# A gated S5 layer on one core: the state kept at every token in place of every second one

## The chip, the cores and the metric

The kernel runs on one core of a Trainium2 chip, in bfloat16 with float32 sums. The core has five engines, each with its own queue that is worked off in order: TensorE (PE, matrix products; PEld is its loading of weights), VectorE (DVE), ScalarE (ACT), GpSimd (POOL) and SyncE (SP, which here issues nearly all DMAs). Waits between engines go by semaphores. The metric is the device time of one execution in microseconds, as the median over several runs.

## The reference

One sequence of 2048 tokens with 448 channels is normalised, goes through a diagonal complex state space (448 complex states), and is gated by a two-layer network with 1792 hidden units.

```python
dt = jnp.exp(log_dt)
Lam_bar = jnp.exp(dt * Lam)
B_bar = ((Lam_bar - 1.0) / Lam)[:, None] * Bmat
Bu = jnp.einsum("bld,pd->blp", x + 0j, B_bar)
h = jnp.zeros_like(Bu[:, 0, :])
for t in range(L):
    h = Lam_bar[None, :] * h + Bu[:, t, :]
    hs.append(h)
hseq = jnp.stack(hs, 1)
y = 2.0 * jnp.einsum("blp,dp->bld", hseq, Cmat).real + x * Dskip[None, None, :]
...
y = _layernorm(x, axis=-1)
h = _gelu(jnp.einsum("bsd,df->bsf", y, w1) + b1)
return jnp.einsum("bsf,fd->bsd", h, w2) + b2
...
xn = _layernorm(x, axis=-1)
s = _A_ref(xn, ...)
g = _silu(_B_ref(xn, ...))
return x + s * g
```

## The kernel before, in words

The tokens are worked in NG = 4 groups of 512, each of two blocks of 256. A group has these stages.

- Norms. VectorE takes mean and variance of each token; `ln_apply` writes the rows `xn_sb` (for the state space) and `xn2_sb` (normalised twice, for the network), and `xt` transposes them, by DMA transposes on SP's queue, into `xnT` and `xn2T`, with the channels on the partitions. The first block of group 0 goes through TensorE instead.
- State inputs, `bu` (L648). The state is kept at every second token only: NK = 256 steps a group, each fed by two tokens, so 2 × 448 = 896 rows in 7 tiles. The input matrix holds B beside Lam·B, which `lb` builds on VectorE with `combine` (L583 to L594), and seven DMA transposes from on-chip memory (`bt`) turn it into `BT`. Per group 49 matmuls at L652; ScalarE moves the sums to `u_sb` (L656 to L660).
- States, `ssm` (L666). The 448 complex states lie on 128 partitions as three tiles with a real and an imaginary part, and the last 64 states as one tile whose halves are the two parts. The rotation of each state is taken out by tables of sines and cosines `WT`, so that what is left is a real recurrence: multiply by the table (L669 to L673), seven scans (L677), cast the result to bfloat16 on ScalarE (L681 to L684), turn it back into `h_sb` (L705 to L709). GpSimd carries the last state over to the next group (L691 to L703).
- Network. `mm1` (L718) is the first layer: 14 tiles of 128 hidden units, 512 tokens wide, in matmuls of 64 rows, two of which are in the array at a time (L726); gelu on ScalarE (L736). In group 0 the first layer runs by blocks of tokens, `mm1_half` (L740), in 112 matmuls of 128 rows and 256 columns (L746), the bias as an extra row of the weights. `mm2` (L756) is the second layer: for each 128 tokens 14 matmuls (L760), then the bias b2 added by VectorE (L763) and silu by ScalarE (L764).
- Output, `ym` (L782). For each 128 tokens of one parity. Even tokens, from the state one step back: seven products with `CZ` (L795) and four with the direct matrix `M0` (L798), which holds the token's own input and the skip term. Odd tokens: seven products with `CQ` (L795, L801), and the skip term `xd`, worked out by `skip` (L766) on VectorE or GpSimd, added by VectorE (L808). Then the gating t3 = s·g (L810), the addition of x (L813), both on VectorE, and a store for each block. `CQ` and `CZ` come from C by `combine`, `M0` from products of CQ and B (`m0`, L628 to L644).

The program is recorded as a list of tasks by a helper, `Plan`. It finds the dependencies, and issues the tasks in an order written out by hand (`ORDER`), each on its engine's queue; for a task recorded by `either`, which has two possible engines, the list `SECOND` says where the second is taken. PSUM banks are fixed in the code.

Of the kernel before, what the change touches and what calls it, by code (L numbers as in the profile page):

```python
# [7 lines left out]
ACT = mybir.ActivationFunctionType  # L8
# [9 lines left out]
class Task:  # L18
# [3 lines left out]
    __slots__ = ("eng", "ins", "reads", "writes", "sem", "idx", "deps", "chain", "alts", "tag")  # L22

    def __init__(self, eng, ins, reads, writes, sem):
        self.eng, self.ins, self.reads, self.writes, self.sem = eng, ins, tuple(reads), tuple(writes), sem
        self.deps = set()
        self.chain = False
        self.tag = None
        self.alts = [(eng, ins)]

    def choose(self, k):
        self.eng, self.ins = self.alts[k]
        if self.sem in ENGS:
            self.sem = self.eng


class Plan:
# [4 lines left out]
    def __init__(self, nc):  # L42
        self.nc = nc
# [19 lines left out]

    def add(self, eng, ins, reads=(), writes=(), dur=0.2, lat=0.1, prio=0.0, sem=None, chain=False, table=None, mode=None):
        if callable(ins):
            ins = [ins]
        t = Task(eng, ins, reads, writes, sem or eng)
        t.chain = chain
        if self.tag is not None:
            t.tag = self.tag  # L70
            self.named[self.tag] = t
            self.tag = None
        self.tasks.append(t)
        return t

    def either(self, first, second, reads=(), writes=(), prio=0.0, chain=False):

        t = self.add(first[0], first[1], reads, writes, chain=chain)
        t.alts.append((second[0], second[1] if isinstance(second[1], list) else [second[1]]))
        return t  # L80

    def dma(self, eng, out_ap, in_ap, reads=(), writes=(), prio=0.0, nbytes=0, transpose=False, dur=0.45):
# [8 lines left out]
        return self.add(eng, fn, reads, writes, sem=sem)  # L91
# [20 lines left out]
    def emit(self):  # L112
# [5 lines left out]
        assert len(order) == len(set(order)) == len(self.tasks)  # L118
        done = {}
# [26 lines left out]

    def settle(self, names):
# [14 lines left out]
ST 0 18 22 10 88 1 19 16 23 15 20 2 21 11 3 9 27 12 26 24 8 17 14 13 25 5 7 6 89 4 28 90 96 91 29 45 30 97 92 98 93 31 46 47 94 99 48 63 103  # L162
95 32 53 100 49 54 101 50 102 33 51 52 114 64 44 106 65 55 38 108 116 56 105 115 39 107 57 109 40 117 58 118 41 120 42 119 36 110 122 34 121
111 37 144 124 35 104 123 43 60 112 62 125 59 B0 126 DH 72 113 67 B1 296 68 69 128 B2 70 127 300 298 73 B3 151 130 129 299 191 148 132 303
131 149 297 134 133 301 302 150 304 136 152 135 142 155 138 66 156 143 153 140 154 137 157 271 139 71 146 308 305 74 165 76 75 141 306 61
309 145 79 307 166 268 82 272 163 BF 83 77 310 86 169 164 181 158 277 269 159 401 180 400 270 170 167 398 147 160 274 W0 W1 W2 405 168 404
182 399 W3 171 280 402 403 183 161 406 172 H10 173 275 162 H11 192 278 184 281 356 174 H12 175 357 185 358 311 78 410 360 80 176 81 H13 361
312 411 229 407 412 408 362 230 409 501 502 H15 363 500 314 188 231 359 315 504 383 189 506 503 H16 232 505 507 508 H14 186 368 178 364 369
187 233 509 365 179 512 366 234 H21 513 177 237 316 H20 367 238 460 313 239 458 510 461 235 242 190 246 373 243 459 245 514 195 193 196 511
236 247 H24 244 H23 194 199 251 466 85 197 200 84 464 198 203 87 249 252 201 253 240 202 241 205 248 204 317 370 206 215 262 217 207 382 318  # L170
218 257 216 258 319 208 254 259 250 D0 263 255 260 209 320 371 256 264 321 210 219 221 D1 220 211 223 265 266 273 222 376 267 413 374 322
224 212 225 D2 326 276 213 227 226 379 325 279 228 214 D3 327 282 331 465 333 323 283 414 285 375 377 332 380 H26 415 334 467 H22 O00 335
470 324 484 462 471 328 289 330 284 416 339 329 286 340 463 261 341 342 H30 290 343 344 417 337 336 292 515 548 418 O01 345 H25 351 516 346
549 H31 485 347 287 348 468 288 293 349 H33 350 550 372 352 338 554 419 378 353 518 354 294 384 291 420 295 421 469 385 387 422 551 423 517
O10 555 388 574 391 389 424 519 428 386 427 475 392 429 437 394 435 425 520 472 426 390 430 436 431 521 432 476 473 481 522 438 O11 433 381
523 440 395 482 447 393 478 434 448 524 575 439 441 442 443 449 450 453 444 451 445 525 446 355 479 452 H32 526 454 H34 455 552 396 556 553
456 397 529 457 H36 557 H35 530 560 531 558 561 539 527 538 559 486 565 483 474 528 487 536 477 535 489 480 534 532 562 537 541 O20 566 533
540 493 488 542 563 544 567 490 564 568 491 494 492 543 545 496 569 546 571 570 O21 495 547 581 572 497 573 578 498 576 O30 499 577 582 579
583 580 584 585 593 589 586 594 595 587 588 590 591 596 592
""".split()]  # L180
SECOND = [int(k) if k.isdigit() else k for k in """
142 143 144 157 163 167 171 173 195 201 219 223 308 309 407 411 413 416 484 485 508 509 512 515 516 518 519 575 W0 W1 W2 595
""".split()]

# [10 lines left out]
def bass_recurrent_scan__ssm_conv_s5__mixer_channel_mlp__prompt_kernel(  # L195
# [14 lines left out]
    NB, NG, NF, NK = 8, 4, 14, 256  # L210
# [3 lines left out]
    with ExitStack() as es:  # L214
        def SB(name, shape, dtype=BF):
# [5 lines left out]
        iota = SB("iota", [128, NK], F32)  # L221
        sgn = SB("sgn", [128, 4], F32)
        cw = SB("cw", [128, 40, 4], F32)
# [3 lines left out]
        dcol = SB("dcol", [128, 8], F32)  # L227
        x_all = SB("x_all", [128, NB, 2, D])
        w1_sb = SB("w1_sb", [128, 4, F])
        w2_sb = SB("w2_sb", [128, NF, D])  # L230
        b1b = SB("b1b", [128, NF])
        b1f = SB("b1f", [128, NF], F32)
        Bn = SB("Bn", [128, 7, 896])
        BT = SB("BT", [128, 7, 7, 128])
        Cr = SB("Cr", [128, 7, D])
        CQ = SB("CQ", [128, 7, D])
        CZ = SB("CZ", [128, 7, D])
        M0 = SB("M0", [128, 4, D])
        dbc = SB("dbc", [128, D])
        xd = SB("xd", [128, 4, D])  # L240
        xr = SB("xr", [128, 2, D], F32)
# [3 lines left out]
        o2 = SB("o2", [128, 4, D], F32)  # L245
        WT = SB("WT", [128, 4, 3, NK])
        xn_sb = SB("xn_sb", [128, 2, 896])
        xn2_sb = SB("xn2_sb", [128, 2, 1024])
        xnT = SB("xnT", [128, 2, 7, 256])
# [8 lines left out]
        pb = SB("pb", [128, 3, 2, NK])  # L258
        v_sb = SB("v_sb", [128, 4, 2, NK])
        s_f = SB("s_f", [128, 4, 2, NK], F32)  # L260
        s_b = SB("s_b", [128, 4, 2, NK])
        h_sb = SB("h_sb", [128, 2, 7, NK + 2])
        Cs = h_sb[0:112, 1, :, :].rearrange("p k c -> p (k c)")[:, 18:530]
# [8 lines left out]
        (LRE, LIM, LDT, DT, F1, A1, R1, R2, F2, DEN, RDEN, LR, LI, NLI, T0, T1, QR, QI, NQR, NQI, ZR, ZI, NZR, NZI,  # L272
         T2, ZT) = range(26)
# [4 lines left out]
        def pool(fn, reads=(), writes=(), dur=0.3, prio=0):  # L278
            kb.add("pool", fn, reads, writes, dur=dur, lat=0.15, prio=prio)

        def dve(fn, reads=(), writes=(), dur=0.2, prio=0):
            kb.add("dve", fn, reads, writes, dur=dur, lat=0.12, prio=prio)

        def act(fn, reads=(), writes=(), dur=0.6, prio=0, table=None):
            kb.add("act", fn, reads, writes, dur=dur, lat=0.2, prio=prio, table=table)

        def pe(fn, reads=(), writes=(), dur=0.2, prio=0):
            kb.add("pe", fn, reads, writes, dur=dur, lat=0.25, prio=prio)

        with nc.Block():  # L290

            S0 = -100
# [636 lines left out]
```

## Time and profile before

| what | us |
|---|---|
| median of 3 runs (range) | 154.56 (154.44 to 154.69) |
| span of the profiled execution | 153.0 |
| TensorE busy | 148.4 |
| VectorE busy | 122.0 |
| ScalarE busy | 110.9 |
| GpSimd busy | 34.8 |

The span is the profiler's, from the first to the last event of the program in that execution; the difference to the median, about 1.5 us, is start and end outside it. The profile names an operation by its line in the code, with its output and inputs: `L677 DVE TENSOR_TENSOR_SCAN` is the scan of line 677 on VectorE. In a group's row stand the count, the sum of busy time, the mean of one in ns, and the engine's idle time ahead of it with what ended it. The clock row (PEclk) gives TensorE's granted clock in tenths.

### The profile page before, as it was taken

The page shows a single profiled execution, that of the slowest core. Times are in us where ns is not written, and L with a number is a line of the kernel's source. Part 1 is how long each engine was busy: PE and PEld are TensorE (multiplying, and loading weights), DVE is VectorE, ACT ScalarE, POOL GpSimd, SP SyncE. Part 2 cuts the span into 40 slices and gives each one's busy share as a digit, 9 for nine tenths or more (in the row PEclk, how much of TensorE's full clock was granted, in tenths as well). Part 3 has the DMA queues.
Part 4 walks back from the last instruction along what each step waited for, and adds up shares of the span by engine and source line. Part 5 has one row for each costly group of instructions (what it writes and reads, how often), then busy time and mean ns, then how long its engine had stood idle before and what let it go on. Part 6 is the DMA issues. An engine that isn't in the chain of part 4 may idle for free.

```text
span 153.0 us, 2971 instructions
## 1 busy us (share of the span) xinstructions
PE 148.4 (97%) x1055; PEld 88.2 (58%) x1055; DVE 122.0 (80%) x262; ACT 110.9 (72%) x190; POOL 34.8 (23%) x115
## 2 busy tenths in 40 slices
PE   7899999999999999999999999999999999999992
PEld 2599965455555555665544456755666555555551
DVE  5785989998957999899898864494976972999564
ACT  3867769999959988699999999832294789661100
POOL 6467491073000060310004310210006000000241
PEclk9999999999999999999999999999999999999999
DMA  4999986999989770000020221131300100001022
GB/s 114 297 324 366 252 185 118 177 125 227 196 143 121 140 137 0 4 0 0 2 50 14 42 78 60 27 38 27 95 4 0 60 0 0 4 0 62 0 107 73
DMA packets 31512, 14.04 MB, mean 92 GB/s; under 512 B 25733, under 2 KB 31113, under 8 KB 31498
## 3 DMA queue, kind: packets, MB, share of 16 engines
q1 hardware_dynamic: 31344, 13.79, 40.1%
q8 instruction: 8, 0.13, 0.3%
q10 hardware_dynamic: 154, 0.07, 0.2%
q14 instruction: 6, 0.05, 0.1%
HBM read 6.20 MB, written 1.84 MB: 53 GB/s over the span
## 4 chain that ended last, share of the span: by engine, by line
PE 94%; DVE 2%; DMA 1%; issue 0%; DVEq 0%
PE psum L760 28%; PE psum L726 21%; PE psum L652 14%; PE psum L795 13%; PE psum L746 8%; PE psum L798 4%; PE psum L631 3%; DMA x_all<-in_A_x_dram 1%; PE psum L801 1%; DVE lnst L395 1%; PE psum L636 1%; PE psum L403 1%; PE psum L466 0%; DVE xn2T L407 0%; DVE t L810 0%
## 5 line engine op out<-in xcount | busy, mean ns | idle before, releaser
L760 PE MATMUL psum<-w_sb,gT 128*128 128x448 bf16 x224 | 44.5, 353 | 0.0
L726 PE MATMUL psum<-xn2T,w_sb 64*128 64x512 bf16 x294 | 33.5, 378 | 0.0
L760 PEld LDWEIGHTS psum<-w_sb,gT 128*128 128x128 bf16 x224 | 21.8, 98 | 19.5 <-issue 0.2
L736 ACT ACTIVATE gT<-psum,b1f 128x512 bf16<-128x512 f32 x42 | 25.9, 690 | 3.1 <-PE psum L726 3.1
L726 PEld LDWEIGHTS psum<-xn2T,w_sb 64*128 64x128 bf16 x294 | 15.6, 109 | 16.3 <-issue 2.3
L652 PE MATMUL psum<-xnT,BT 128*128 128x256 bf16 x196 | 24.1, 273 | 0.0
L652 PEld LDWEIGHTS psum<-xnT,BT 128*128 128x128 bf16 x196 | 18.5, 98 | 6.4 <-issue 3.1
L677 DVE TENSOR_TENSOR_SCAN s_f<-cw,cur,v_sb 128x256 f32<-128x256 f32 x21 | 15.1, 740 | 0.2
L451 ACT ACTIVATE xn_sb<-x_all,lnw 128x448 bf16<-128x448 bf16 (+1 forms) x21 | 13.4, 667 | 1.2 <-POOL lnw L428 1.2
L764 ACT ACTIVATE g_sb<-o 128x448 bf16<-128x448 f32 x16 | 8.9, 572 | 6.4 <-DVE o L763 6.2
L746 PE MATMUL psum<-xn2T,w_sb 128*128 128x256 bf16 x112 | 12.7, 273 | 0.4 <-DVE xn2T L407 0.4
L746 PEld LDWEIGHTS psum<-xn2T,w_sb 128*128 128x128 bf16 x112 | 11.9, 111 | 0.9 <-issue 0.8
L795 PE MATMUL psum<-CZ,h_sb 128*128 128x448 bf16 x56 | 11.9, 353 | 0.0
L810 DVE TENSOR_TENSOR t<-psum,g_sb 128x448 bf16<-128x448 f32 (+2 forms) x10 | 5.7, 574 | 7.6 <-PE psum L798 3.8
L656 ACT ACTIVATE u_sb<-psum 128x512 bf16<-128x512 f32 x12 | 7.1, 593 | 5.9 <-PE psum L652 5.8
L763 DVE TENSOR_TENSOR o<-psum,b2bc 128x448 f32<-128x448 f32 x16 | 9.7, 614 | 1.5 <-PE psum L760 1.5
L795 PE MATMUL psum<-CQ,h_sb 128*128 128x448 bf16 (+2 forms) x54 | 10.5, 332 | 0.0
L752 ACT ACTIVATE gT<-psum 128x512 bf16<-128x512 f32 x14 | 8.2, 593 | 3.2 <-PE psum L746 3.1
L381 DVE BATCH_NORM_STATS2 lnst<-x_all 128x6 f32<-128x448 bf16 x14 | 8.3, 610 | 0.6 <-DMA x_all<-in_A_x_dram 0.5
L590 ACT ACTIVATE tmp<-Cr,cw 128x448 f32<-128x448 bf16 (+1 forms) x12 | 7.9, 672 | 1.0 <-DVE CQ L593 0.9
L691 POOL TENSOR_TENSOR cwk<-s_f,ang 128x3 f32<-128x3 f32 x3 | 1.1, 352 | 32.6 <-DVE s_f L677 32.5
L795 PEld LDWEIGHTS psum<-CZ,h_sb 128*128 128x128 bf16 x56 | 5.4, 98 | 4.9 <-issue 0.4
(157 smaller groups left out, 212.0 us busy)
## 6 DMA issues: line engine op xcount, KB each, us to landing
out_dram<-tmp SPq DMA_DIRECT2D x7, 224.0 KB, 1.9
x_all<-in_A_x_dram SPq DMA_DIRECT2D x3, 448.0 KB, 4.5
w_sb<-in_B_w_dram SPq DMA_DIRECT2D x3, 448.0 KB, 6.6
w_sb<-in_B_w_dram SPq DMA_DIRECT2D x3, 384.0 KB, 4.6
Bn<-in_A_B_im_dram SPq DMA_DIRECT2D x1, 336.0 KB, 9.3
Bn<-in_A_B_re_dram SPq DMA_DIRECT2D x1, 336.0 KB, 9.8
x_all<-in_A_x_dram SPq DMA_DIRECT2D x2, 112.0 KB, 2.1
x_all<-in_A_x_dram SPq DMA_DIRECT2D x1, 224.0 KB, 3.7
```

Source lines behind the costliest of these rows:

```text
L381: dve([lambda e, b=b, par=par, q=q: e.bn_stats(lnst[:, q, :], x_all[:, 2 * g + b, par, :])], [f"x{2 * g + b}"] + (["xmT0p1"] if (g, b) == ...
L451: ("act", [lambda e, o=o, i=i: e.activation(o, i, ACT.Identity, bias=nb, scale=rs) for o, i in pairs], 0.75, 0.2)]
L652: fns = [lambda e, r=r, m=m, d=d: e.matmul(psum[:, 4, r * NK:(r + 1) * NK], BT[:, m, d, :], xnT[:, gx, d, :], start=(d == 0), stop=(d == 6 ...
L677: dve(lambda e, i=i, ri=ri, init=init: e.tensor_tensor_scan(s_f[:, i, ri, :], col(R2, i).to_broadcast([128, NK]), v_sb[:, i, ri, :], init, ...
L726: return lambda e: e.matmul(psum[:, b0 + k, :], w1_sb[halves[h], d, fcol(2 * j + k)], rhs[halves[h], d, :, :], start=first and d == 0, sto ...
L736: act([lambda e, k=k: e.activation(gT[:, gb, 2 * j + k, :], psum[:, b0 + k, :], ACT.Gelu_apprx_tanh, bias=b1f[:, 2 * j + k:2 * j + k + 1]) ...
L746: fns = [lambda e, k=k, d=d: e.matmul(psum[:, banks[k], :].rearrange("p (r c) -> p r c", r=2)[:, :, cs], w1_sb[:, d, fcol(2 * j + k)], rhs ...
L752: act(lambda e: e.activation(gT[:, 0, 2 * j:2 * j + 2, :].rearrange("p k (r c) -> p k r c", r=2)[:, :, :, cs], psum[:, b0:b0 + 2, :].rearr ...
L760: fns = [lambda e, fi=fi: e.matmul(psum[:, bk, 0:D], gT[:, gb, fi, q * 128:(q + 1) * 128], w2_sb[:, fi, :], start=(fi == 0), stop=(fi == N ...
L763: dve(lambda e: e.tensor_tensor(o2[:, ob, :], psum[:, bk, 0:D], b2bc[:], ALU.add), [f"ps{bk}", "b2bc"], [f"oo{ob}"], 0.62, prio - 76)
L764: act(lambda e: e.activation(g_sb[:, gs, :], o2[:, ob, :], ACT.Silu), [f"oo{ob}"] + (["silu"] if g == 0 else []), [f"g{gs}"], 0.58, prio - ...
L795: fns = [lambda e, k=k: e.matmul(psum[:, bk, c0:c1], h_sb[:, hb, k, k0:k0 + 128], cm[:, k, c0:c1], start=(k == 0), stop=False) for k in ra ...
```

## The change

The state is kept at every token: NK = 512 steps a group. With that there is no Lam·B (`lb`), no second output matrix `CZ`, no `M0`, and no separate skip term: every block of 128 tokens has seven products with `CQ` and four small ones with a diagonal matrix `DG` (128 columns each), which add the skip term in PSUM. The recurrence uses R1, the decay of one token, in place of R2.

```diff
-    NB, NG, NF, NK = 8, 4, 14, 256
+    NB, NG, NF, NK = 8, 4, 14, 512
...
-                fns = [lambda e, k=k: e.matmul(psum[:, bk, c0:c1], h_sb[:, hb, k, k0:k0 + 128], cm[:, k, c0:c1], start=(k == 0), stop=False)
-                       for k in range(7)]
-                if par == 0:
-                    fns += [lambda e, d=d: e.matmul(psum[:, bk, c0:c1], xnT[:, gx, d, xs], M0[:, d, c0:c1], start=False, stop=(d == 3)) for d in range(4)]
...
+                    fns = [lambda e, k=k: e.matmul(psum[:, bank.b, c0:c1], h_sb[:, hb, k, k0:k0 + 128], CQ[:, k, c0:c1], start=(k == 0), stop=(k == 6))
+                           for k in range(7)]
+                    ds = [d for d in range(4) if c0 <= d * 128 < c1]
+                    fns[1:1] = [lambda e, d=d: e.matmul(psum[:, bank.b, d * 128:min(D, d * 128 + 128)], xnT[:, gx, r * 4 + d, xs], DG[:, d, 0:min(128, D - d * 128)],
+                                                        start=False, stop=False) for d in ds]
```

The state inputs have 448 rows in place of 896, in four tiles of rows. For the three full tiles the matmuls are of 64 rows and 512 columns, two in the array at a time, as in the first layer (a shared helper, `halved`); the fourth tile of channels holds its 64 rows twice, so that each half has them, for which `xn_sb` and `x_all` are padded to 512 columns (extra loads `ldxe`, and copies on GpSimd, `dup`). The last 64 states' inputs are two halves of the array's columns, real and imaginary, over all rows.

```diff
+            def halved(out, wt, rhs, n, tag, rd, bank):
+                def half(k, d, h):
+                    first = h == k
+                    return lambda e: e.matmul(out(k), wt(k, d, halves[h]), rhs(k, d, halves[h]),
+                                              start=first and d == 0, stop=not first and d == 2)
+                own = [half(k, d, k) for d in range(4) for k in range(2)]
+                other = [half(k, d, 1 - k) for d in range(3) for k in (1, 0)]
...
+                    def colhalf(d, k):
+                        h = slice(0, 128 if d < 3 else 64)
+                        return lambda e: e.matmul(psum[halves[k], bank.b, :], BT[h, d, k * D + 384:k * D + D], xr[h, d, :, :], start=(d == 0), stop=(d == 3))
+                    pe([colhalf(d, k) for d in range(4) for k in range(2)], rd, [bank.key], rows(4, 512))
```

B is transposed by six DMA transposes, four straight from HBM and two for its last 64 columns from a buffer `Bs`, after a copy on GpSimd.

```diff
+            def bt():
+                for n in range(2):
+                    for ri, bm in enumerate((A_B_re, A_B_im)):
+                        kb.dma("sp", BT[:, 0:3, ri * D + n * 224:ri * D + n * 224 + 224], dram_ap(bm, n * 224 * D, [[D, 224], [1, 384]]),
+                               writes=[f"BT{ri}{n}"], nbytes=172032, transpose=True)
+                for ri in range(2):
+                    tail = Bs[:, ri, :].rearrange("p (t c) -> p t c", t=4)
+                    pool(lambda e, tail=tail: e.tensor_copy(tail[:, :, 64:128], tail[:, :, 0:64]), [f"Bs{ri}"], [f"Be{ri}"], 0.45)
+                    kb.dma("sp", BT[:, 3, ri * D:ri * D + D].rearrange("p (t r) -> p t r", t=4), Bs[:, ri, :], reads=[f"Bs{ri}", f"Be{ri}"], writes=[f"BT{ri}2"], nbytes=114688, transpose=True)
```

The first layer of group 0 uses `halved` too (196 matmuls of 64 rows and 256 columns), with its bias in the activation. The addition of x is recorded with two engines for every block; `SECOND` puts 14 of the 17 on GpSimd (17, as the last 128 tokens are split in two parts).

```diff
-                fns = [lambda e, k=k, d=d: e.matmul(psum[:, banks[k], :].rearrange("p (r c) -> p r c", r=2)[:, :, cs],
-                                                    w1_sb[:, d, fcol(2 * j + k)],
-                                                    rhs[:, d, :, :], start=(d == 0), stop=(d == 3))
-                       for k in range(2) for d in range(4)]
...
+                halved(lambda k: psum[:, bank.b + k, :].rearrange("p (r c) -> p r c", r=2)[:, :, cs], lambda k, d, h: w1_sb[h, d, fcol(2 * j + k)],
+                       lambda k, d, h: xr[h, d, :, :], 256, f"H0{j}{b}", (["xmT0p0", "xmT0p1"] if b == 0 else ["xmT0_1"]) + [f"w1_{c}", f"w1r_{c}"], bank)
...
-                    if last and par:
-                        kb.either(*on, rd, [f"o{ob}_{par}_{c0}"], prio)
-                    else:
-                        dve(add, rd, [f"o{ob}_{par}_{c0}"], on[0][2], prio)
...
+                    on = [("dve", add, 0.15 + 0.25 * w / D), ("pool", add, 0.2 + 1.0 * w / D)]
+                    kb.either(*on, rd, [f"o{ob}_{r}_{c0}"])
```

Several buffers share memory now: the table of token numbers lies in `pb`, the tail of B in `s_b`, C in `h_sb`. The buffer of second-layer sums, `o2`, has two places in place of four. PSUM banks are handed out by a list, `BANKS`, in the order of first use, with the waits that follow from it (`place`). A block's rows are contiguous tokens now, not alternate ones. `ORDER` has 593 tasks in place of 640 and is new throughout, as are `SECOND` and `BANKS`.

More of the change, by code (lines that the diff above doesn't have):

```diff
@@ L118, in emit @@
         assert len(order) == len(set(order)) == len(self.tasks)
+        self.place(order)
         done = {}
@@ L716, in fcol, with mm1 @@
                 return slice(a * 128 + fi - a, (a + n) * 128, n)
[L718 removed]
+            def mm1(g, j):
                 gx, gb = g % 2, g % 2
[L720 to L736 removed]
@@ L831, in bass_recurrent_scan__ssm_conv_s5__mixer_channel_mlp__prompt_kernel @@
-            P = {"ln": -9, "bu": -8, "mm1": 0, "mm2": 5, "ym": 6}
-            def pr(k, g, x=0.0):
-                return P[k] + 10 * g + x
+                if r and not last:
+                    kb.dma("sp", dram_ap(out, off, [[D, 128], [256 * D, 2], [1, D]]), o_sb[:, ob, :].rearrange("p (r d) -> p r d", r=2),
+                           reads=[f"o{ob}_0_0", f"o{ob}_1_0", f"o{ob}_1_256"], writes=[f"out{g}{b}"], nbytes=229376)
+            idle = kb.psum()
+            kb.tag = "I0"
+            pe([lambda e: e.matmul(psum[:, idle.b, :], still[:, :], still[:, None, :].to_broadcast([128, 4, 128]), start=True, stop=True) for _ in range(8)],
+               ["still"], [idle.key], 3.4)
```

823 lines of the change are left out of this document (384 added, 439 removed), and 3 rows, old and new, of the table ORDER.

## The prediction

> **What bounds the kernel now.** I read the page's totals first, then the two kinds of busy rows by slice, then the chain that ended last.
>
> ```profile
> span 153.0 us, 2971 instructions
> PE 148.4 (97%) x1055; PEld 88.2 (58%) x1055; DVE 122.0 (80%) x262; ACT 110.9 (72%) x190; POOL 34.8 (23%) x115
> PE   7899999999999999999999999999999999999992
> DVE  5785989998957999899898864494976972999564
> PEclk9999999999999999999999999999999999999999
> PE 94%; DVE 2%; DMA 1%; issue 0%; DVEq 0%
> PE psum L760 28%; PE psum L726 21%; PE psum L652 14%; PE psum L795 13%; PE psum L746 8%; PE psum L798 4%; PE psum L631 3%; DMA x_all<-in_A_x_dram 1%; PE psum L801 1%; DVE lnst L395 1%; PE psum L636 1%; PE psum L403 1%; PE psum L466 0%; DVE xn2T L407 0%; DVE t L810 0%
> ```
>
> TensorE is busy in every slice but the first and the last, at full granted clock, and holds 94% of the chain: its matmuls end to end are the time. VectorE is 31.0 us short of the span and has slack in the slices with 4 to 7. Whatever leaves TensorE shortens the kernel, until VectorE, with 80%, has more than its slack put on it. Both happen here.
>
> **TensorE, part by part.** The chain's pieces (start, us) give what a matmul takes of the path.
>
> ```profile
> 7.22 5.40 PE psum L746 x48
> 12.62 0.45 PE psum L466 x8
> 13.06 7.11 PE psum L746 x64
> 41.19 3.13 PE psum L726 x28
> 60.70 1.32 PE psum L631 x7
> 70.38 0.79 PE psum L636 x14
> 73.92 1.32 PE psum L795 x7
> 105.41 0.76 PE psum L652 x7
> 124.93 0.87 PE psum L652 x7
> 149.92 0.12 PE psum L801
> ```
>
> The direct matrix M0 goes: three products of 1.32 and one of 0.79, −4.75. The output stage now takes 13+4+1% of 153.0, 27.5 us. After, each of 16 blocks is seven matmuls, 1.32, and four diagonal ones of 128 columns (0.45/8 = 0.056 each), 0.22: 16 × 1.54 = 24.7, −2.8. The first layer of group 0 takes 5.40 + 7.11 = 12.51; it becomes 196 half-row matmuls of 256 columns. No such row exists; L636, halves of 224 columns, takes 0.79/14 = 56 ns, the half-row of 512 columns 3.13/28 = 112 ns. So 56 ns, 11.0 us, −1.5; if two halves did not share the array it would be 111 ns (7.11/64), 21.8 us, +9.2. L726 and L636 both show the sharing, so I keep 56. The state inputs are 28 runs of seven at 0.76 to 0.87, 21.3 to 24.4, and their share of 14% says that they stand at the low end, some 22; after, per group 42 half-row matmuls and 8 column halves at 112 ns, 5.6, in all 22.4: I take +0.2. The column halves have only L636 for a row; unshared they would add 8 × 0.11 = 0.9 a group. Each change from half rows back to the full array costs 0.87 − 0.76 = 0.11. Sum: −4.75 − 2.8 − 1.5 + 0.2 = −8.9. Were TensorE still the bound, the span would be 144.1.
>
> **VectorE, part by part.** The state pass now handles 512 steps a group where it handled 256.
>
> ```profile
> L669 DVE TENSOR_TENSOR pa<-u_sb,WT 128x1536 bf16<-128x1536 bf16 x4 | 3.8, 955 | 2.2 <-ACT u_sb L656 2.1
> L672 DVE TENSOR_TENSOR pa<-u_sb,WT 128x512 bf16<-128x512 bf16 x4 | 1.7, 416 | 2.7 <-ACT u_sb L660 2.7
> L677 DVE TENSOR_TENSOR_SCAN s_f<-cw,cur,v_sb 128x256 f32<-128x256 f32 x21 | 15.1, 740 | 0.2
> 129.67 2.03 DVE L677 TENSOR_TENSOR_SCAN s_f<-cw,cur,v_sb 128x256 f32<-128x256 f32 x3
> L563 DVE SCALAR_TENSOR_TENSOR s_f<-iota,cw,s_f 128x256 f32<-128x256 f32 x4 | 1.7, 474 | 0.0
> L566 DVE SCALAR_TENSOR_TENSOR s_f<-s_f 128x1024 f32<-128x1024 f32 x1 | 1.2, 1224 | 0.0
> L763 DVE TENSOR_TENSOR o<-psum,b2bc 128x448 f32<-128x448 f32 x16 | 9.7, 614 | 1.5 <-PE psum L760 1.5
> L593 DVE SCALAR_TENSOR_TENSOR CZ<-Cr,cw,tmp 128x448 bf16<-128x448 bf16 x7 | 4.7, 679 | 0.0
> L593 DVE SCALAR_TENSOR_TENSOR Bn<-Bn,cw,tmp 128x448 bf16<-128x448 bf16 x7 | 4.7, 671 | 0.0
> L808 DVE TENSOR_TENSOR xr<-psum,xd 128x448 f32<-128x448 f32 x7 | 4.3, 611 | 2.9 <-PE psum L801 2.9
> ```
>
> Six wide operations a group go from 1536 to 3072 elements: the slope (955 − 416)/1024 gives 0.526 ns an element, so 0.955 + 0.81 = 1.76. The scan: fixed part from L563 and L566, 474 − 256 × 0.977 = 224 ns; the rest of 740, 516 ns, doubles: 1.26 (bounds 0.74 and 1.48). Three scans in 2.03 stand 0.645 apart, so 512 steps stand about 1.16 apart; neighbours overlap by 0.06 to 0.1 us in general. The small pair of operations becomes 0.69 and 0.42. That is per group 6 × 0.8 + 7 × 0.52 + 0.4 = 8.9 more, 35 in all. Removed: the 14 combines for CZ and Lam·B with most of their scaled copies (9.4 and more), the skip sums (4.3), and 14 adds that go to GpSimd (next part). VectorE comes to some 133 to 135 us of work, as much as TensorE's, and unlike TensorE's it is a chain with a start: no state pass can begin before the first state inputs.
>
> [...]
>
> **The start of that chain.** B now comes by six transposes on SP's queue, behind the transposes of the normalised rows.
>
> ```profile
> 19.65 1.33 SPq L89 DMA_TRANSPOSE xnT<-xn_sb  x1
> 26.08 2.59 SPq L89 DMA_TRANSPOSE BT<-Bn  x2
> 30.22 3.46 SPq L89 DMA_TRANSPOSE BT<-Bn  x2
> BT<-Bn SPq DMA_TRANSPOSE x7, 3.9
> L656 ACT ACTIVATE u_sb<-psum 128x512 bf16<-128x512 f32 x12 | 7.1, 593 | 5.9 <-PE psum L652 5.8
> ```
>
> One transpose of B goes ahead; then SP stands at the first transpose of normalised rows until they are ready, 19.65 now, and I take 20.0. Behind it stand three of B, the second block's rows and the last two of B: six issues of 1.30 (2.59/2) later, at 27.8, the last one goes out and lands 3.9 after that, 31.7. The last two state-input tiles (28 halves, 3.1) need it, and their evacuation by ScalarE (two of 0.593) follows: VectorE's first wide operation starts at 36.0. TensorE has the first layer and the second of group 0 up to about 29 meanwhile, so 31.7 is SP's doing. At 3.46 for two, the bound above, the last lands 3 us later, and so does all that follows. The two transposes of the tail also wait for GpSimd's copies, small and early; behind all of them on SP stand group 1's rows, C's transposes and the extra 64-column loads of x, which the combines and the first output block need only after the scans.
>
> From there to the last state of group 3, VectorE in its new order executes 24 wide operations at 1.70 net of overlap (40.8), 28 scans at 1.16 (32.5), 8 of 0.63 and 8 of 0.38 (8.1), 10 gatings like L810 and 8 b2 adds like L763 at 0.54 (9.7), 7 combines at 0.60 (4.2), and 1.9 of normalisation: 97.2. ScalarE's cast of the scans, twice its size, lies in each group beside 3 us and more of gatings, b2 adds and the small scan; I cost it at nothing, and if that cover is gone it is some 3 us a group. So 36.0 + 97.2 = 133.2 if VectorE never waits.
>
> **What the adds cost on GpSimd.** The add of x moves there for 14 of 17 pieces (16 blocks, the last in two). The rows that show both engines at once:
>
> ```profile
> 98.52 0.62 DVE L810 TENSOR_TENSOR t<-xr,g_sb 128x448 bf16<-128x448 f32 x1
> 98.66 1.38 POOL L775 TENSOR_TENSOR xd<-xn_sb,dbc 128x448 bf16<-128x448 bf16 x1 [9.86 <-DVE xr L808]
> 99.18 1.10 DVE L813 TENSOR_TENSOR tmp<-t,x_all 128x448 bf16<-128x448 bf16 x1
> L813 DVE TENSOR_TENSOR tmp<-t,x_all x15: 366/383/1104, 82.2 to 149.6; 128x448 bf16<-128x448 bf16 x15
> 144.62 1.09 POOL L775 TENSOR_TENSOR xr<-xd,g_sb 128x448 f32<-128x448 bf16 x1 [23.33 <-ACT g_sb L764]
> 144.74 0.62 DVE L808 TENSOR_TENSOR xr<-psum,xd 128x448 f32<-128x448 f32 x1
> 114.56 0.53 POOL L700 TENSOR_TENSOR cwk<-cwk,ang 128x1 f32<-128x1 f32 x1 [14.52 <-ACT cwk L699]
> 116.21 0.19 POOL L702 TENSOR_TENSOR cwk<-s_f,ang 128x1 f32<-128x1 f32 x1
> ```
>
> The add at 99.18, median 0.383, took 1.10, and ended within 0.3 us of GpSimd's product: it stood still until GpSimd let go, 0.72 lost. The one at 144.74, which reads PSUM, lost nothing. The other way round GpSimd's small product took 0.53 beside a scan, 0.19 alone. So an add on GpSimd, about 1.0 alone, delays the VectorE operation with two SBUF operands that is issued after it. In the new order 10 of the 14 adds fall before the last state, and by their places about 8 stand ahead of a wide operation or a scan, the others ahead of operations on PSUM. At 0.8 each (0.72 and the next one's start) that is 6.4; GpSimd's 30 small products for the carried state add 0.7, by two or three that meet a wide operation at the 0.53 − 0.19 of L700. On GpSimd's own queue the carry products stand behind adds too, at up to three adds, but the scan that reads the carry comes after three wide operations (5.1), which cover it. Bounds: 0, and 10 × 1.0 + 30 × 0.1 = 13. I take 7.1, since the only row with the same operands has a price near the full one: last state at 140.3.
>
> [...]
>
> **The end.** After the last state, four output blocks on TensorE (1.54 each, 6.2 with the last one split), then what follows TensorE's last matmul now: 153.0 − 150.04 = 3.0. 140.3 + 6.2 + 3.0 = 149.5. The runs' median lies 1.5 over the profiled span (154.56 − 153.0): **151.0 us, 2.3% faster**, with VectorE and not TensorE as the bound.
>
> **The rivals.** B, the lock is hidden: adds on GpSimd fall in VectorE's waits. Then 133.2 + 9.2 = 142.4 for VectorE, under TensorE's 144.1; with 1.4 us of changes of array mode and waits for the first transposes, 145.5 and a median of 147.0. For it: L808's undisturbed 0.62, and slack in slices of 4 to 7. Against: VectorE has little slack left.
>
> C, slower: the lock at its full price. All 10 adds and the 30 small products delay VectorE, 13 us in place of 7.1: 133.2 + 13 + 9.2 + 1.5 = 156.9. It decides as soon as VectorE loses over 10.7 us, by this or by a late cast that waits behind a locked scan. For it: 1.10 at 99.18, and six wide operations of 1.76 a group that can meet an add. Against: L808's 0.62.
>
> D, the prices themselves: scans at the bound of 1.48 give 28 × 0.22 = 6.2 more, 157.2; half rows not shared give more than that. Against: L563's fixed part and L636. It has the same sign as C and is held with it.
>
> E, the change does not bring its 8.9 us on TensorE because TensorE waits in every group for states, and ends with VectorE where it did: 154.5.
>
> **How the numbers follow.** Forecast 0.45 (149 to 154), B 0.23, C with D 0.26, E 0.06. About 0.2% (0.3 us) is what a measurement of this kernel can tell from no change. Faster: forecast and B, less the upper edge, 0.66. Slower: C, D and half of E, 0.29; the rest, 0.05, same. The range reaches down to B's 147.0 less the uncertainty of its waits, 146.5, and up to D, 157.5.
>
> **What would show it.** Right: TensorE below 95% with idle time before its output blocks, released by VectorE's states; VectorE's lines heading the chain; wide operations of 1.76 and scans near 1.26; the first wide one near 36, the last small state add near 140; wide operations and scans longer than their median whenever an add runs on GpSimd, and that add well over 1 us. Wrong: the state inputs over 5.7 us a group or the half rows of 256 columns over 56 ns (TensorE's sum); the first wide operation later than 38 (SP's queue); scans near 1.48; an add on GpSimd that leaves VectorE's medians alone (then B); VectorE idle before the state operations, waiting for ScalarE's cast (then the cover I gave it is missing).

## The result, and the profile after

| | median us | span of the profiled execution | ratio to before, 95% interval |
|---|---|---|---|
| before (4 runs beside it) | 154.62 | 153.0 | |
| changed | 166.22 (164.67 to 168.11) | 162.9 | 1.0646 (1.056 to 1.0731) |

The changed kernel is 6.5% slower. Two of the four runs of the changed kernel (167.32 and 168.11, against 164.67 and 165.12) and the profiled one of the first experiment (161.62, against 158.41 to 158.65) count as slow, and the ratios leave such runs out. First its page, the totals and the rows by slice, then the chain's shares.

```profile
span 162.9 us, 3030 instructions
PE 143.9 (88%) x1140; PEld 77.5 (48%) x1140; DVE 140.0 (86%) x195; ACT 121.9 (75%) x184; POOL 75.0 (46%) x120
PE   7674599992999999999999899899995999999492
DVE  2860179986569998999999999999999999999984
PEclk9969999999699999999999999999999999999999
DMA  5633899347998790000038300000810010001013
DVE 54%; PE 10%; SPq 8%; ACT 8%; DMA 7%; POOL 5%; issue 5%; DVEq 0%; ACTq 0%
```

Two things are to be seen. From slice 13 on VectorE is full and holds 54% of the chain, as the prediction had it: the bound has moved from TensorE to VectorE. But ahead of that, in slices 1 to 12 (up to 49 us), VectorE isn't full, and stands nearly still from 12 to 20 us; TensorE is at 4 to 7 tenths up to slice 5 and at 2 in slice 10, where the kernel before had it at 9 from its third slice on. The time by stage shows which of the two is the miss. VectorE's rows for the first wide operation and the last small state sum, on its timeline (start, us):

```profile
48.25 1.76 DVE L700 TENSOR_TENSOR pa<-u_sb,WT 128x3072 bf16<-128x3072 bf16 x1 [0.29 <-ACT u_sb L683]
153.13 0.42 DVE L742 TENSOR_TENSOR h_sb<-pa 128x512 bf16<-128x512 bf16 x1
```

| stage | predicted us | measured us |
|---|---|---|
| until VectorE's first wide operation | 36.0 | 48.25 |
| from there to the last state | 97.2 + 7.1 = 104.3 | 153.55 − 48.25 = 105.3 |
| from there to the end | 9.2 | 162.9 − 153.55 = 9.35 |

So 12.25 of the 13.4 us between the predicted span, 149.5, and the measured one lie ahead of the first wide operation. The 7.1 in the second row is the price of what the prediction calls the lock: time that VectorE's operations lose beside GpSimd's additions and small products (0.72 us for the addition at 99.18 in the kernel before). The chain of waits in the first stage (start, us):

```profile
4.60 2.83 SPq L107
7.47 2.68 SPq L107
10.20 1.51 SPq L107
11.75 8.29 DMA w_sb<-in_B_w_dram
21.16 3.13 ACT gT L767 x8
24.29 0.11 ACT ang L560
24.48 0.85 POOL ang L551
29.38 2.28 POOL ang L556
32.61 0.37 POOL s_b L643
33.61 0.34 POOL s_b L643
34.23 1.28 SPq L106
36.88 3.63 DMA xnT<-xn_sb
```

And SP's rows for the loads of w1, the first transpose of B and the last one, on its timeline:

```profile
2.18 10.83 SPq L107 DMA_DIRECT2D w_sb<-in_B_w_dram  x8
22.88 3.12 SPq L106 DMA_TRANSPOSE BT<-in_A_B_re_dram  x1
39.58 1.28 SPq L106 DMA_TRANSPOSE BT<-in_A_B_im_dram  x1
```

The chain reads: SP takes 2.83 and 2.68 us over two issues, where the loads ahead of them took 0.42 to 0.70; a piece of w1 lands only at 20.04; TensorE and so the gelus are late; behind eight gelus on ScalarE stands one step of 0.2 us for the sine polynomial, which runs at 24.2; GpSimd works off the ten steps of the polynomial from 24.5 until 32.0, and behind that, in its queue, stand the two copies of B's tail (L643), which end at 33.0 and 34.0. SP waits 4.5 us with a transpose for the first copy, until 33.0, and with it wait all the transposes behind; the second copy is ready by the time that SP comes to it. Two causes are in this chain: a slow load, and a short copy in a long queue.

### The profile page after: what moved, and what is told of

Its sections match the earlier page's. It is cut to its first block, busy times and chain, and to the rows that moved or that the text cites. A ratio compares the mean times of both kernels' runs of the same rounds, so it can differ in the third digit from the quotient of the medians.

```text
span 162.9 us, 3030 instructions
## 1 busy us (share of the span) xinstructions
PE 143.9 (88%) x1140; PEld 77.5 (48%) x1140; DVE 140.0 (86%) x195; ACT 121.9 (75%) x184; POOL 75.0 (46%) x120
## 4 chain that ended last, share of the span: by engine, by line
DVE 54%; PE 10%; SPq 8%; ACT 8%; DMA 7%; POOL 5%; issue 5%; DVEq 0%; ACTq 0%
DVE s_f L708 17%; PE psum L666 6%; SPq L107 6%; DMA w_sb<-in_B_w_dram 5%; DVE pb L739 5%; DVE pa L738 5%; DVE h_sb L740 4%; ACT gT L755 4%; DVE pa L700 4%; DVE t L807 4%; DVE v_sb L702 3%; DVE pb L701 3%; PE psum L801 3%; DVE CQ L633 2%; DVE o L786 2%
## 5 line engine op out<-in xcount | busy, mean ns | idle before, releaser
L666 PE MATMUL psum<-xn2T,w_sb 64*128 64x512 bf16 (+1 forms) x490 | 46.7, 342 | 8.2 <-DMA w_sb<-in_B_w_dram 6.3
L666 PEld LDWEIGHTS psum<-xn2T,w_sb 64*128 64x128 bf16 x490 | 28.1, 110 | 25.2 <-DMA w_sb<-in_B_w_dram 6.6
L809 POOL TENSOR_TENSOR tmp<-t,x_all 128x448 bf16<-128x448 bf16 x14 | 23.1, 1665 | 31.9 <-issue 17.6
L708 DVE TENSOR_TENSOR_SCAN s_f<-cw,cur,v_sb 128x512 f32<-128x512 f32 x21 | 29.4, 1448 | 0.1
L801 PE MATMUL psum<-CQ,h_sb 128*128 128x448 bf16 (+2 forms) x119 | 24.9, 342 | 2.7 <-DVE h_sb L742 2.7
L666 PE MATMUL psum<-xnT,BT 64*128 64x512 bf16 x168 | 21.1, 395 | 4.0 <-DMA xnT<-xn_sb 3.1
L787 ACT ACTIVATE g_sb<-o 128x448 bf16<-128x448 f32 x16 | 9.0, 572 | 11.2 <-DVE o L786 11.1
L767 ACT ACTIVATE gT<-psum,b1f 128x256 bf16<-128x256 f32 x28 | 11.1, 484 | 8.0 <-PE psum L666 8.0
L713 ACT ACTIVATE s_b<-s_f 128x3072 bf16<-128x3072 f32 x4 | 11.2, 2788 | 6.0 <-DVE s_f L708 6.0
L683 ACT ACTIVATE u_sb<-psum 128x1024 bf16<-128x1024 f32 x12 | 11.9, 1046 | 2.5 <-PE psum L666 2.5
L499 ACT ACTIVATE xn_sb<-x_all,lnw 128x512 bf16<-128x512 bf16 x16 | 12.7, 815 | 0.2
L807 DVE TENSOR_TENSOR t<-psum,g_sb 128x448 bf16<-128x448 f32 (+2 forms) x17 | 9.9, 585 | 0.6 <-PE psum L801 0.5
L786 DVE TENSOR_TENSOR o<-psum,b2bc 128x448 f32<-128x448 f32 x16 | 9.4, 609 | 0.0
```

The costliest lines, as they stand in the source:

```text
L499: ("act", lambda e: e.activation(dst, src, ACT.Identity, bias=nb, scale=rs), 0.81)]
L666: return lambda e: e.matmul(out(k), wt(k, d, halves[h]), rhs(k, d, halves[h]), start=first and d == 0, stop=not first and d == 2)
L683: act(lambda e: e.activation(u_sb[:, i, :, :], psum[:, bank.b:bank.b + 2, :], ACT.Copy), [bank.key], [f"u{i}"], 1.02)
L708: dve(lambda e, i=i, ri=ri, init=init: e.tensor_tensor_scan(s_f[:, i, ri, :], col(R1, i).to_broadcast([128, NK]), v_sb[:, i, ri, :], init, ...
L713: act(lambda e: e.activation(s_b[:, 0:3, :, :], s_f[:, 0:3, :, :], ACT.Copy), SF, ["sb"] + early, 2.76)
L786: dve(lambda e: e.tensor_tensor(o2[:, ob, :], psum[:, bank.b, 0:D], b2bc[:], ALU.add), [bank.key, "b2bc"], [f"oo{ob}"], 0.62)
```

## The experiments

**The load that reads its source twice, and the copies.** The changed kernel loads the last 64 rows of w1 into both halves of the partitions by one load whose source has a first dimension of 2 with step 0. The first experiment puts two plain loads of 64 rows in its place; the matmuls then wait for both, in lines that are not printed here.

```diff
-                ld("sp", w1_sb[:, 3, a:a + w], dram_ap(B_w1, 384 * F + a, [[0, 2], [F, 64], [1, w]]), [f"w1r_{c}"], 128 * w * 2, dur=0.55)
+                ld("sp", w1_sb[0:64, 3, a:a + w], dram_ap(B_w1, 384 * F + a, [[F, 64], [1, w]]), [f"w1r_{c}"], 64 * w * 2)
+                ld("sp", w1_sb[64:128, 3, a:a + w], dram_ap(B_w1, 384 * F + a, [[F, 64], [1, w]]), [f"w1s_{c}"], 64 * w * 2)
```

> The last 64 rows of w1 are loaded by two plain loads of 64 rows for each chunk in place of one load that reads its source twice. Theory of the late start, first half (the load that reads its source twice is slow and holds SP's queue: two of its neighbours' issues take 2.83 and 2.68 us, and TensorE waits 6.3 us for w1): TensorE's first layer ends near 20 in place of 26.8, ScalarE's step of the sine polynomial runs near 17 in place of 24.2, GpSimd's copies of B's tail end near 26.5 in place of 34, the first wide operation starts near 42 in place of 48.2; span near 156.5, time near 158.3. Rival, the half-row matmuls or the number of loads set that end: first layer still ends past 25, span within 1 us of 162.9. Rival, the time is lost in VectorE's stretch (the lock): the start may move, but the span stays above 160.

Measured: first wide operation at 43.56, 158.65 us, ratio 1.0228 (1.0136 to 1.032). TensorE's first layer ends at 20.6, ScalarE's step runs at 17.9, GpSimd's copies end at 27.7, and SP's last transpose of B goes out at 33.26, 6.3 earlier than in the changed kernel. The start came within 1.6 of what the theory had and the time within 0.4; both rivals fall. The start is that of the profiled execution, which took 161.62: its granted clock was 0.968 in the mean, and its 42 half rows of state inputs took 7.90, where four other versions, at 0.995 to 1.000, took 4.95. So the 4.7 us by which the start came earlier is less than what the load costs.

The second moves GpSimd's copies of B's tail (tasks 155 and 157 of `ORDER`) ahead of the polynomial (55).

```diff
-53 54 55 56 62 H001 254 ...
+53 54 155 157 55 56 62 H001 254 ...
```

> GpSimd's two copies of B's tail stand ahead of the ten steps of the sine polynomial in place of behind them; nothing else. Theory of the late start, second half (SP stands 4.5 us at a transpose that waits for a copy queued behind that polynomial): SP's transposes go on at 28.5 in place of 33.0, the first wide operation starts near 43.7 in place of 48.2, span near 158.4, time near 160.2. Rival, another wait takes its place (ScalarE's tables, which end near 40, or VectorE's norms): start moves by less than 1.5 us and the span stays above 161.4.

Measured: first wide operation at 45.82, span 159.8, 162.33 us, ratio 1.045 (1.0356 to 1.0543). SP no longer stands at the transpose of the tail. Its timeline in the changed kernel, where the transpose that begins at 33.01 waited for 4.5 us:

```profile
27.28 1.23 SPq L106 DMA_TRANSPOSE xnT<-xn_sb  x1
33.01 1.19 SPq L106 DMA_TRANSPOSE BT<-s_b  x1
```

and here:

```profile
27.51 1.23 SPq L106 DMA_TRANSPOSE xnT<-xn_sb  x1
28.86 1.20 SPq L106 DMA_TRANSPOSE BT<-s_b  x1
```

So the copies did cost SP 4.4 us; 2.4 of them reached VectorE's start. The start came 2.1 later than the theory had and the time 2.1 higher, between theory and rival. What bounds it there is TensorE: its first layer still waited for w1, the second layer of group 0 ends only at 37.7, and the evacuation of the state inputs by ScalarE at 45.6. Both edits together:

> Both edits together. Theory of the late start: what the prediction had wrong is the start alone, so with both out of the way the first wide operation starts near 37, as the prediction had it (36.0), the stretch from there to the last state stays near 105 us, and the span comes to 151.7, time near 153.5, about 0.7% under the kernel before. Rival, ScalarE's tables or TensorE's second layer bound the start at 40 or later: span 155 or more, time 156.7. Rival, the lock grows with more overlap: the stretch takes 108 us or more.

Measured: first wide operation at 38.78, the stretch to the last state 106.1, span 154.2, 155.77 us, ratio 1.0035 (0.9993 to 1.0077), which is no difference from the kernel before. The theory's start of 37, span of 151.7 and time of 153.5 were missed by about 2 us each. The two edits give back 9.5 of the 12.25 us. By the ratios, the load alone takes off 4.2 points, the copies alone 2.0, both 6.1: within the intervals they add up. The rest of the start, 2.8, was not in the theory (more on it below).

**Why that load is slow.** One load of the same bytes from 128 different rows.

```diff
-... dram_ap(B_w1, 384 * F + a, [[0, 2], [F, 64], [1, w]]) ...
+... dram_ap(B_w1, 320 * F + a, [[F, 128], [1, w]]) ...
```

> The changed kernel with one edit: the load of w1's last rows is one load of 128 different rows (320 to 447) in place of one that reads 64 rows twice; the same bytes, packets and number of loads. The lower half of that tile then holds other rows of w1, so the first layer is not the reference's. Theory: the load that reads its source twice has 2 as its outermost count and so keeps only 2 of the 16 DMA engines busy (the DMA row shows 1 to 2 tenths there). Then TensorE's wait of 6.3 us for w1 falls under 2, the long issues of 2.83 and 2.68 us on SP go, and the start and the time are as with two loads: first wide operation near 43.5, span near 158.3. Rival, the bytes or the size of the packets make it slow: the wait stays at 6 us and the span within 1 us of 162.9.

The busy times by stretch for the changed kernel and, below it, for this run (columns: TensorE, its loading, VectorE, ScalarE, GpSimd with counts, granted clock, DMA share, GB/s):

```profile
7.43:10.15 2.72, 0.83 (x10) 0.64 (x11) 2.34 (x14) 1.06 (x1) 2.33 (x12) 0.86 0.14 46
10.15:13.03 2.88, 2.33 (x22) 1.43 (x18) 1.00 (x3) 0.51 (x2) 1.21 (x4) 0.54 0.63 175
```

```profile
7.43:10.15 2.72, 2.72 (x52) 2.43 (x48) 2.34 (x14) 2.50 (x6) 2.33 (x12) 1.00 1.09 329
10.15:13.03 2.88, 2.88 (x52) 2.54 (x50) 2.20 (x6) 2.88 (x8) 0.99 (x4) 1.00 1.08 368
```

While SP was held for 2.68 us, the DMA engines were busy to 0.14, about 2 of 16, and moved 46 GB/s; in the same stretch of the run with 128 rows, in which later loads are under way already, the share is 1.09, at 329 GB/s. TensorE's first layer, by form, before and after the edit:

```profile
L666 PE MATMUL psum<-xn2T,w_sb 64*128 64x256 bf16 x196 | 13.1, 291 | 6.3 <-DMA w_sb<-in_B_w_dram 6.3
```

```profile
L674 PE MATMUL psum<-xn2T,w_sb 64*128 64x256 bf16 x196 | 11.2, 270 | 0.0
```

The wait of 6.3 us is gone. The half rows take 270 ns in place of 291: in the changed kernel the granted clock was 0.50 from 9.40 to 12.82, and the slowest of them took 417. Time 155.99, ratio 1.0077 (1.0057 to 1.0098), first wide operation at 39.72. VectorE's row for it, and SP's for the loads of w1, first with two loads a chunk and then here:

```profile
2.20 7.14 SPq L107 DMA_DIRECT2D w_sb<-in_B_w_dram  x12
```

```profile
2.20 4.03 SPq L107 DMA_DIRECT2D w_sb<-in_B_w_dram  x8
39.72 1.76 DVE L708 TENSOR_TENSOR pa<-u_sb,WT 128x3072 bf16<-128x3072 bf16 x1
```

The start is 3.8 us earlier than with two loads, and the expectation of 158.3 was too high. Four issues fewer account for 2.0 of the 3.8: SP reaches the first transpose of normalised rows at 18.94 in place of 20.98. For the rest there is the lower clock of that profiled execution (0.968 in the mean, 0.989 here), whose half rows of state inputs took 7.90 in place of 6.52 here.

This is the largest single effect on record. With nothing but the access pattern changed, and the copies left where they were, the start moves from 48.25 to 39.72, 8.5 of the 12.25 us, the span from 162.9 to 154.7, and the time gives back 5.7 of the 6.5 points. So the lateness of the copies follows for the most part from the load: the polynomial starts at 16.1 in place of 24.5, though SP still stands 3.7 us for the first copy.

That the bytes don't make the load slow is shown, for they are equal, and the wait went from 6.3 us to 0.0; nor does reading the same rows twice, for the two plain loads of the first experiment read them twice as well, and there too the wait fell, to 1.5. What is left is the pattern, a first dimension of 2 with step 0. No run separates the count of 2 from the step of 0: the theory's choice of the count was the author's estimate, which the share of 0.14, 2.2 of 16 engines, fits but does not prove. SP's rows show besides that the loads behind it on the queue are held: the eight issues took 10.83 us in place of 4.03.

**The additions on GpSimd.** In the changed kernel's trace the scan that starts at 112.77, beside an addition on GpSimd that starts at 112.65, took 2.06 us, where the median of such scans is 1.27; and the addition that starts at 93.82, beside a wide operation from 93.99 and a scan from 95.66, took 2.81, where the shortest took 1.03. What this costs in all is seen from the version with both edits, with the 14 additions taken back to VectorE (out of `SECOND`, and each right behind its gating in `ORDER`).

> Both edits, and the 14 additions of x that GpSimd has run on VectorE, each right behind its gating. The prediction's price of the lock (0.8 for 8 of 10 additions ahead of the last state, 6.4 us) against what they cost on VectorE (10 of 0.38 to 0.5, 3.8 to 5.0): the stretch from the first wide operation to the last state 1.4 to 2.6 us shorter than in the run with both edits, span 0.5 to 2.6 us less. Full price (10 us): 5 us less or more. No price (rival B of the prediction): 4 us more.

Measured: stretch 103.6 in place of 106.1, span 151.7, 153.43 us, ratio 0.9891 (0.9829 to 0.9953), as expected. Scans and the additions by form, with the additions on GpSimd:

```profile
L718 DVE TENSOR_TENSOR_SCAN s_f<-cw,cur,v_sb 128x512 f32<-128x512 f32 x21 | 29.4, 1449 | 0.0
L819 POOL TENSOR_TENSOR tmp<-t,x_all 128x448 bf16<-128x448 bf16 x14 | 23.2, 1668 | 32.5 <-DVE t L817 24.5 <-issue 8.0
L710 DVE TENSOR_TENSOR pa<-u_sb,WT 128x3072 bf16<-128x3072 bf16 x4 | 7.8, 1959 | 0.0
```

and on VectorE:

```profile
L718 DVE TENSOR_TENSOR_SCAN s_f<-cw,cur,v_sb 128x512 f32<-128x512 f32 x21 | 25.5, 1265 | 0.1
L819 DVE TENSOR_TENSOR tmp<-t,x_all 128x448 bf16<-128x448 bf16 x15 | 5.9, 393 | 0.5
L710 DVE TENSOR_TENSOR pa<-u_sb,WT 128x3072 bf16<-128x3072 bf16 x4 | 7.0, 1759 | 0.4 <-ACT u_sb L693 0.3
```

The scans lose 3.9 us to GpSimd and this wide line 0.8; L748 and L749 lose 0.8 each likewise (1928 and 1954 against 1736 and 1749 ns). That is 6.3 us, against 6.4 in the prediction, for work that costs VectorE about 4 (ten additions of 0.39). GpSimd loses time too: an addition takes 1.67 in the mean, where the shortest in the changed kernel took 1.03.

The same edit on the changed kernel as it is:

> The changed kernel with its late start, and the 14 additions of x on VectorE. If the lock costs what the scans and wide operations show with additions on GpSimd (21 scans at 1.449 against 1.265, three wide lines at 1.95 against 1.75, 6.3 us in all) and the ten additions cost 0.43 each on VectorE, the stretch from the first wide operation (48.2) to the last state shrinks from 105.3 to near 103, span near 160.5. No price of the lock: 4 us longer than before, span 166. Full price of 10 us: span under 158.

Measured: span 163.9, 163.92 us, ratio 1.0623 (1.0583 to 1.0662), which cannot be told from the changed kernel's. This is a miss in size: VectorE's busy time in the stretch falls from 103.7 to 101.4, as expected, but it stands idle 3.0 us ahead of its combines for CQ, more than the 0.8 it did, and the stretch stays at 105.5. The trace shows where the wait comes from, step by step back. The combines wait for a scaled copy by ScalarE, which starts at 63.17 in place of 60.84 in the changed kernel; ScalarE's table load and gelus ahead of it are 2.3 later as well (53.76 against 51.43); and those follow TensorE, which waited 2.60 us, until 50.25, for a transpose of normalised rows (`xn2T`) that landed 7.0 us after its issue, where it went on at 47.91 in the changed kernel. Why this transpose landed late stays open. The price of the lock is seen alike in both runs (the scans take 1266 ns here and 1448 in the changed kernel, 1265 and 1449 in the pair with both edits); that taking it away gains time is shown only where the start is mended.

**What sets the start now.** One more of B's transposes ahead of the first transpose of rows (task 154 ahead of 135), on top of the version with both edits and the additions on VectorE.

> The version with both edits of the start and the additions on VectorE, and one more of B's transposes from HBM ahead of the first transpose of normalised rows, where SP stands idle for 1.8 us. Theory of the start (the last transpose on SP's queue sets it): first wide operation 1.3 earlier, near 36.8, the prediction's 36.0, span near 150.4, time near 152.1. Rival, the rows' own transposes or ScalarE set the start: no change, within 0.4 us of 151.7.

Measured: span 151.1, 152.87 us, ratio 0.9864 (0.9837 to 0.9891), but the first wide operation at 38.24, 0.1 later: the rival by the start, though the span fell by 0.6. And with four loads for w1's last rows in place of eight:

> As the version with the early transpose, but w1's last rows come by four loads in place of eight (two of 64 rows for the first chunk, two for all the others). The run with the same bytes in one load started VectorE's chain 3.8 us earlier than the one with two loads for each chunk, with four issues fewer. Theory (SP's issues set the start): SP reaches the first transpose of rows about 2 to 3 us earlier, first wide operation near 36, stretch 102.9, span near 148.8, time near 150.6. Rival (TensorE's first and second layer of group 0, or ScalarE's tables, set the start by now): within 0.5 us of 151.1.

Measured: first wide operation at 39.00, span 151.7, 153.06 us, ratio 0.9883 (0.9863 to 0.9903): no gain either, with four issues fewer. SP's last transpose of B and TensorE's first matmuls of state inputs, in the version with the additions on VectorE and both edits:

```profile
29.55 1.28 SPq L106 DMA_TRANSPOSE BT<-in_A_B_im_dram  x1
31.82 4.95 PE L676 MATMUL psum<-xnT,BT 64*128 64x512 bf16 x42
36.16 1.94 ACT L693 ACTIVATE u_sb<-psum 128x1024 bf16<-128x1024 f32 x2 [0.62 <-PE psum L676]
```

and with the four loads:

```profile
28.64 1.28 SPq L106 DMA_TRANSPOSE BT<-in_A_B_im_dram  x1
32.51 4.95 PE L678 MATMUL psum<-xnT,BT 64*128 64x512 bf16 x42
```

SP is 0.9 us earlier and TensorE 0.7 later. TensorE turns to the state inputs only when the second layer of group 0 is through, near 32, needs 5 us for them, and ScalarE one more: 38. SP has ceased to set it. In the run with the four loads there is a second chain beside this one, on VectorE itself:

```profile
34.62 0.41 DVE L510 TENSOR_SCALAR xn_sb<-x_all,lnw 128x512 bf16<-128x512 bf16 x1 [2.19 <-ACT xn_sb L511]
36.91 2.17 DVE L437 BATCH_NORM_STATS2 lnst<-x_all 128x6 f32<-128x448 bf16 x4
39.00 1.75 DVE L712 TENSOR_TENSOR pa<-u_sb,WT 128x3072 bf16<-128x3072 bf16 x1
```

VectorE waits 2.19 us for normalised rows from ScalarE, then works without a gap through its norms up to the first wide operation; the state inputs were ready at 38.81, 0.2 before. The version with both edits shows the same (a wait of 2.25, then no gap, with the state inputs ready at 38.59). With SP out of the way these two chains reach the start within 0.3 us of each other, so that shortening one alone would gain little; no run shortens either.

**b2 on TensorE.** For five blocks b2 comes by one more matmul, and silu reads PSUM (`B2_PE`, which the changed kernel leaves empty).

```diff
-B2_PE = ()
+B2_PE = (8, 9, 10, 11, 12,)
```

> As the last, and for five of the 16 blocks (all of group 2, the first of group 3) b2 is added by one more matmul of TensorE, and silu reads PSUM: five operations of 0.54 leave VectorE's chain ahead of the last state, and TensorE gets 5 of 0.19. If VectorE's chain is the bound: 2.7 us less, span near 147.7, time near 149.4. If TensorE has become the bound (its busy time 142.5 and the start): under 1 us less or slower.

Measured: span 151.5, 153.16 us, ratio 0.9903 (0.9879 to 0.9926), the second case: VectorE's busy time in the stretch falls by 2.0, but the stretch is 102.1 in place of 102.85, and TensorE is busy for 99.2 of it. With both the four loads and four such blocks:

> The same, with b2 of group 2's four blocks added by TensorE. The run with five such blocks shortened the stretch by 0.8 and lengthened the tail by 0.7, which speaks for TensorE as an equal bound (busy 99.2 of 102.1 us of that stretch). So near the run before it: within 0.6 us, either way. If VectorE were the bound alone it would be 2.2 us less.

Measured: span 150.2, 152.16 us, ratio 0.983 (0.9811 to 0.9849), the fastest version, 1.7% under the kernel before. It is 0.9 us under the one with four loads alone, more than the 0.6 expected either way and less than the 2.2 of a bound by VectorE alone. As five such blocks gained nothing on their own (153.16 against 152.87), what b2 on TensorE is worth stays open within 1 us.

## Why the prediction was wrong, step by step

- TensorE's sum held. Its busy time at full clock was 140.4 (in the version with the early transpose) against 148.4 − 8.9 = 139.5; the first layer's 196 half rows took 11.2 where the prediction had 11.0.
- VectorE's prices held: wide operations of 1.75 for 1.76, small ones of 0.67 and 0.42 for 0.69 and 0.42, the scan alone 1.21 for 1.26. So rival D falls; E falls too, as TensorE's sum held and VectorE became the bound.
- The lock held: 6.3 for 6.4. Scans and wide operations lost time beside GpSimd's additions; the operations that read PSUM did not, for L807 and L786 take 612 and 609 ns in the changed kernel, and 614 and 612 (as L815 and L794) with the additions on VectorE. Rival C had the sign but not the cause; its full price of 13 was not paid. Rival B fell. That the stretch came out at 105.3 for 104.3 is in part luck: without the lock it is 103.6, of which the ten additions on VectorE are about 4, so its base was 99.6 and not 97.2, while the lock cost less than the 7.1 that the sum has with the small products.
- The end held: 9.35 for 9.2. The profiled execution's time, 164.67, lies 1.8 over its span in place of 1.5.
- **The start failed: 36.0, measured 48.25.** Two steps of it made most of the miss. "SP stands at the first transpose of normalised rows until they are ready, 19.65 now, and I take 20.0": it was 27.28. SP itself came free only at 26.0, behind its held loads and the first transpose of B, and then waited for rows from ScalarE until 27.26, behind gelus that waited for w1. The prediction costed the first layer's matmuls and put the new form of the load that feeds them at nothing, without a reason. "The two transposes of the tail also wait for GpSimd's copies, small and early": small, but not early; they stand in GpSimd's queue behind a polynomial that itself waits for ScalarE, and ended at 33.0 and 34.0. These two cost 7.3 and 4.5 us on SP's queue, and 27.8 + 7.3 + 4.5 = 39.6: SP's last transpose of B went out at 39.58. By experiment the load alone gives back 8.5 us of the start, both 9.5.
- What is left, 2.8, is what the prediction did not have ahead of the start. SP's last transpose of B went out at 29.37 in place of 27.8 with both edits, and VectorE's own norms, behind rows from ScalarE, fill the time up to 38.78, as shown above. ScalarE's last two evacuations took 1.92 together where the prediction had two of 0.593. And "TensorE has the first layer and the second of group 0 up to about 29 meanwhile": it was 30.7 with both edits, and near 32 in the versions after, where all 42 half rows follow, not the last 28.
- The bounds then failed as well: the range let the start move by 3 us (slower issues of transposes), and said that it shifts the end by as much, but gave it no rival of its own, though it named a first wide operation later than 38, by SP's queue, as a sign that it is wrong. With the measured start in place of 36.0 the prediction's own sum gives 149.5 + 12.25 + 1.5 = 163.3, against 164.67 of the profiled execution.

## What to carry to other kernels

A bound that moves to an engine with a chain brings in a new term, the start of that chain, and time lost ahead of it is lost at the end (here, with one load changed, the start came 8.5 us earlier and the span 8.2): follow each queue that leads to it, task by task, as one follows the bound itself. A load with a changed access pattern is a changed operation even when its bytes are few: look at the DMA share while it runs (0.14 here, 1.09 with the same bytes in another pattern), and at what is queued behind it (eight issues in 10.83 us in place of 4.03). A short operation is early only if what stands ahead of it in its engine's queue is (the two copies here take 0.37 and 0.34 us, and ended at 33.0 and 34.0).

## What the runs showed of the hardware that was not expected

- While the changed kernel's loads of 128 KB whose source begins with a dimension of 2 were under way, from 7.43 to 10.15, the DMA engines stood at a share of 0.14 and 46 GB/s, against 1.09 and 329 in the same stretch with loads of the same bytes from 128 rows, and two issues on SP took 2.83 and 2.68 us, where loads ahead of them took 0.42 to 0.70.
- In the changed kernel TensorE's granted clock was 0.50 from 9.40 to 12.82 and from 40.12 to 43.54, and 1.00 otherwise. Each stretch begins near a wait of TensorE (2.41 us up to 9.32, and 3.15 us up to 40.65), but another wait of 2.33 us, up to 17.58, passed at 1.00, so the cause stays open. What it costs is seen in the half rows: 291 ns in the mean against 270 in the first layer, and 6.23 us for the 42 half rows of state inputs against 4.95.
- GpSimd lost time beside VectorE as well, on tiny operations too: in the changed kernel its products of 128x3, 0.19 at their shortest, took up to 1.75 beside wide operations (L728 at 101.32, beside L701 from 101.26 to 103.02; the three at L728 1.20 in the mean).
